# When the output projection's weights are loaded and split: rounds 1 to 5 of the last pair instead of rounds 12 and 13

## The chip, the cores and the metric

The kernel runs on one core of one Trainium2 chip. The metric is device time in microseconds (us) of one execution; of several runs the median is compared. TensorE does the matrix products, VectorE (DVE), ScalarE (ACT) and GpSimd (POOL) the elementwise work, and the sequencer of SyncE (SP) issues nearly all transfers in the order of one queue: an issue that has to wait holds up those behind it.

## The reference

Two branches work on the same `x` of 2048 tokens by 640 features and are mixed by a gate for each token.

```python
g = sigmoid((x * gate_w).sum(-1, keepdims=True))
# A: Fourier mixing, the real part of a DFT over features and then over the sequence
a = einsum("bsd,ed->bse", x, dft_hid_re); b = einsum("bsd,ed->bse", x, dft_hid_im)
A = einsum("ts,bse->bte", dft_seq_re, a) - einsum("ts,bse->bte", dft_seq_im, b)
# B: attention with 32 heads of 20 features, one shared k and v
q = (x @ wq) in 32 heads; k = x @ wk; v = x @ wv
B = concat_heads(softmax(q k^T / sqrt(20)) v) @ wo
out = g * A + (1 - g) * B
```

All data are fp32. The product of this study's concern is the last one of B, `@ wo`, with weights of 640 by 640.

## The kernel before

**Splitting.** Exact products are made out of faster ones: an fp32 operand is split into a rounded high part and the remainder, the low part, and a product becomes three matmuls, high by high, high by low and low by high (`mm3`, L114 to L116). Every operand that is streamed this way has to be split first, by one CAST and one TENSOR_TENSOR.

**Stages.** The kernel first projects `q`, `k`, `v` and the gate, then does the hidden DFT. Then comes the long part: heads are worked through in 16 pairs (`NPAIR`), and between the attention's matmuls TensorE gets those of the sequence DFT. A pair has score maxima (`a`, L330, reduced by VectorE at L337), scores (`b`, L785, with the exponential on ScalarE at L795) and the weighted sum of `v` (`av`, L799). The order of all this is written out as a string, `PLAN`, for 15 pairs. The last pair has no maxima left for a successor, and its order is a loop of 16 rounds, `kk` = 0 to 15. At the end stands the output projection: 32 groups `o_group`, one for each block of 128 tokens and half of the features, 15 matmuls each, with the two weight parts `wos` and the split attention output `ospl`.

**The sequence DFT in the last pair.** It is made of seven products of half-sized matrices (`PRODUCTS`), each in eight groups of output rows, 56 groups `g` in all (`GROUPS`). A group takes the sequence matrix in two halves, `sh` = 0 and 1. For a half, `load_c` fetches a raw block `craw` of 128 by 1024 (two where the product takes a sum) and `split_c` makes `ch` and `cl` of it (L463, L464), on VectorE for groups 49 to 55. Groups 48 to 55 fall into the last pair, one half a round. In the middle of half (g, sh) the half (g+1, sh) is split, two rounds ahead of its use; so round 12 splits (55, 0) and round 13 (55, 1), which TensorE uses in rounds 14 and 15. When a group has ended, ScalarE copies the two sums out (`y_evict`, L685), and GpSimd adds them (L707) and combines them with earlier results (`ya`, L712), which go back to `y_d`.

**The output projection's preparation.** It hangs on a table, `BEFORE`, whose functions are called behind a round:
- `load_wo(cs)`: for each block `c` of 128 rows of `wo`, a load into a buffer `xr0` or `xr1` (by turns, those that the DFT's `load_x` used before), then the CAST and TENSOR_TENSOR on VectorE (L567, L568) into `ab0` to `ab4`, the places of an operand of the product before;
- `load_o(n)`: a quarter of the last pair's half of tokens: attention sums `oT_d` and reciprocal softmax sums `rx_d`; `mult_o(n)` multiplies them on GpSimd (L590); `split_o(n)` splits the result on VectorE (L606, L607);
- `load_y(tb)`: rows of the finished Fourier branch for the mixing, into buffers that `craw`, `ch` and `cl` leave.

**What sets the order.** For TensorE, ScalarE, VectorE and GpSimd the order of issue is the order of the code (`manual_schedule`). SP's queue is not in that list: the framework orders the transfers by its own plan, so a load can stand earlier than its line, and it waits there until its buffer is free. All waits between engines are semaphores.

**The last half's sums.** `finish_half` writes a half's attention sums and softmax sums to memory, `finish_last` reads the softmax sums back, takes the reciprocals on VectorE (L845) and sends them out and in again for `mult_o`.

Of the kernel before, what the change touches and what calls it, by code (L numbers as in the profile page):

```python
# [22 lines left out]
KC = D // P  # L23
NT = S // P
# [10 lines left out]
def kernel(  # L35
# [69 lines left out]
    def move(dst, src, queue=nc.sync):  # L105
        queue.dma_start(words(dst), words(src))  # L106
# [262 lines left out]
    def tick():  # L369
        clock["n"] += 1  # L370
        due = [t for t in todo if t[0] <= clock["n"]]
        todo[:] = [t for t in todo if t[0] > clock["n"]]
        for _, f, args in due:
            f(*args)
# [182 lines left out]
    def spare(k, name):  # L557
        tag, n = SPARE[k % 4]
        return cpools[n].tile([P, D], F32, tag=tag, name=name)

    def load_wo(cs):
        for c in cs:
            raw = xp.tile([P, D], F32, tag=f"xr{c % 2}", name="woraw")
            move(raw, wo[c * P : (c + 1) * P])
            t = abp.tile([P, 2, D], F32R, tag=f"ab{c}0", name=f"wo{c}")
            split_w = (t[:, 0], t[:, 1])
            nc.vector.tensor_copy(split_w[0], raw)  # L567
            nc.vector.tensor_tensor(split_w[1], raw, split_w[0].bitcast(F32), op=ALU.subtract)  # L568
            wos[c] = split_w
# [5 lines left out]
    def load_o(n):  # L575

        if n < NO:
            oraw[n] = []
            for k, v in enumerate((oT_v, rx_v)):
                if (n % 2, k) == (1, 1):  # L580
                    t = op.tile([P, KC, TW], F32, name="oraw", bufs=1)
                else:
                    t = abp.tile([P, KC, TW], F32, tag=f"ab{5 + 2 * (n % 2) + k}0", name="oraw")
                move(t, v[:, :, n * TW : (n + 1) * TW])
                oraw[n].append(t)

    def mult_o(n):
        if n < NO:
            o, r = oraw[n]
            nc.gpsimd.tensor_tensor(o, o, r, op=ALU.mult)  # L590

    def split_o(n):
        if n < NO:
            if n % 4 == 0:

                h, l = [
                    qbuf[(LAST + 1 + k) % 3][:, : KC * TW].rearrange("p (c t) -> p c t", c=KC)
                    for k in range(2)
                ]
            else:  # L600
                h, l = [
                    abp.tile([P, KC, TW], F32R, tag=f"ab{2 * (n % 4 - 1) + k}1", name="osp")
                    for k in range(2)
                ]
            o = oraw.pop(n)[0]
            nc.vector.tensor_copy(h, o)  # L606
            nc.vector.tensor_tensor(l, o, h.bitcast(F32), op=ALU.subtract)  # L607
            ospl[n] = (h, l)

    def load_y(tb):  # L610
        if tb < NT:
            yrow[tb] = spare(tb, "yrow")
            move(yrow[tb], y_d[tb * P : (tb + 1) * P])
# [61 lines left out]
    def y_evict():  # L675

        if not ended:
            return
        grp = ended[0]
        ps = grp["ps"]  # L680
        if "t" not in grp:
            grp["t"] = [op.tile([P, HALF], F32, name=("yt", "yu")[k]) for k in range(len(ps))]
            grp["left"] = list(range(len(ps)))
        k = grp["left"].pop(0)
        nc.scalar.activation(grp["t"][k], ps[k], AF.Copy)  # L685
        if not grp["left"]:
            ended.pop(0)
            y_out(grp)
# [153 lines left out]
    def finish_last(ts, sm):  # L842
# [107 lines left out]
    STEPS = [(p, qh, kc) for p in range(NPAIR) for qh in range(2) for kc in range(NT)]  # L950

    BEFORE = {
        4: (lambda: load_wo(range(3)), lambda: load_o(0), lambda: load_o(1)),
        5: (lambda: load_wo(range(3, KC)), lambda: mult_o(0), lambda: mult_o(1)),
        6: (lambda: split_o(0), lambda: load_o(2)),
        7: (lambda: [load_y(tb) for tb in range(4)],),
    }
    LAG = 2
    taken["V"] = LAG
# [1 line left out]
    def next_b(g, tag):  # L961
        r, nb = divmod(taken["b"][g], 4)
        p, qh, kc = STEPS[2 * r + nb // 2]
        b_unit(p, g, kc, 2 * qh + nb % 2, tag)
        taken["b"][g] += 1
        ready()

    def next_v():
        st = taken["V"] - LAG
        taken["V"] += 1  # L970
        if st >= 0:
            av_step(*STEPS[st])
            if STEPS[st][2] == NT - 1:
                finish_half(*STEPS[st][:2])
# [23 lines left out]
    for kk in range(NT):  # L998
        block = 2 if kk in (0, NT - 1) else 4 * (kk % 2)
        at = (1, 5, 9, 13) if block else (0, 6, 12, 18)  # L1000
        for i in range(24):
            if i in at:
                tick()
                for g in range(2):
                    next_b(g, f"S{lrot % 5}")
                    lrot += 1
            halves.run(0)
            if i == 23:
                y_evict()
            halves.run(1)  # L1010
        y_evict()
        for _ in range(block):
            next_v()
        for f in BEFORE.get(kk - NT // 2, ()):
            f()
    old = STEPS[-LAG:]
    for _ in range(2):
# [6 lines left out]
    for i in range(2 * NT):  # L1024
        tb, e = divmod(i, 2)
# [63 lines left out]
```

## Time and profile before

| what | value |
|---|---|
| median of 3 runs | 1782.73 us (1782.6 to 1783.92) |
| profiled execution | 1780.08 us |
| its span, first to last instruction | 1778.3 us |
| TensorE busy | 1768.7 us, 99% |
| VectorE busy | 1429.6 us, 80% |
| ScalarE busy | 1186.8 us, 67% |
| GpSimd busy | 823.6 us, 46% |
| granted TensorE clock | 1.000 |

Rows of a timeline give the start in us from the span's beginning, the time to the end of the last merged instruction, engine, line, operation, names as output<-input, shapes and count; brackets hold the idle time just before and what ended it. A row of waits gives who waited for whom, the total in us, how often, and the longest. Matmuls are pipelined, so consecutive rows of TensorE overlap. In the last pair the rounds 0 and 1 begin near 1597 us, and every two rounds after them take 12.70 us, but for the last two.

### The profile page before, as it was taken

Reading aid. Unit: us, or ns where it says so; the run is one execution under the profiler, and the core shown is the slowest. Engines: PE = TensorE matmul, PEld = TensorE weight load, DVE = VectorE, ACT = ScalarE, POOL = GpSimd, SP = SyncE. Lnnn points to the kernel's source line nnn. Section 1 sums busy time; section 2 is a strip of 40 time slices with the busy share of each in tenths; the row PEclk is TensorE's granted clock in tenths of the full one; section 3 lists DMA queues with packets and bytes.
Section 4 is the critical chain, followed back from the end, with each engine's and each line's share of the span. In section 5 each row is a group of like instructions: output and inputs, shape, how many; then the busy total and the mean of one; then the engine's idle time right before and its main releaser. Section 6 shows DMA issues by size and latency. Waiting matters only on the chain.

```text
span 1778.3 us, 40733 instructions
## 1 busy us (share of the span) xinstructions
PE 1768.7 (99%) x16342; PEld 1265.7 (71%) x16342; DVE 1429.6 (80%) x2335; ACT 1186.8 (67%) x2327; POOL 823.6 (46%) x559
## 2 busy tenths in 40 slices
PE   9999999999999999999999999999999999999999
PEld 7799986666666666666666666666666666667789
DVE  5479998888888888888888888888888888843364
ACT  5422247777777777777777777777777777777631
POOL 1011127544456464657655556565654444342332
PEclk9999999999999999999999999999999999999999
DMA  8663324342434432535443434342433242325566
GB/s 277 224 196 101 110 98 143 97 131 86 141 110 137 126 126 93 172 117 161 131 162 119 140 113 153 106 152 98 153 122 122 71 144 75 103 73 173 194 216 222
DMA packets 131002, 243.88 MB, mean 137 GB/s; under 512 B 26356, under 2 KB 77556, under 8 KB 128292
## 3 DMA queue, kind: packets, MB, share of 16 engines
q1 hardware_dynamic: 130012, 238.00, 41.5%
q0 software_dynamic: 800, 3.28, 0.6%
q8 instruction: 128, 2.10, 0.5%
q14 instruction: 62, 0.51, 0.1%
HBM read 194.62 MB, written 50.86 MB: 138 GB/s over the span
## 4 chain that ended last, share of the span: by engine, by line
PE 94%; issue 2%; DMA 2%; POOL 1%; DVE 1%; SPq 0%; ACT 0%; POOLq 0%; DVEq 0%; ACTq 0%
PE av L799 26%; PE y L656 19%; PE a L330 17%; PE b L785 16%; PE ab L125 8%; PE o L114 1%; PE q L114 1%; PE q L116 1%; PE o L116 1%; PE o L115 1%; PE q L115 1%; POOL ya L712 1%; DMA craw<-in_cre_dram 0%; DMA y_d<-ya 0%; SPq L106 0%
## 5 line engine op out<-in xcount | busy, mean ns | idle before, releaser
L337 DVE TENSOR_REDUCE mx<-a 128x1 f32<-128x512 f32 x2048 | 1264.6, 681 | 172.1 <-PE a L330 118.2
L795 ACT ACTIVATE pt<-b 128x512 f32<-128x512 f32 x2048 | 1052.3, 620 | 334.7 <-PE b L785 200.0
L656 PE MATMUL y<-x,ch 64*128 64x320 f32 x3584 | 756.6, 309 | 0.7 <-ACT yt L685 0.7
L330 PE MATMUL a<-ks,qs 60*128 60x512 f32 x2048 | 741.0, 423 | 0.3 <-ACT half L533 0.3
L785 PE MATMUL b<-qs,ks 62*128 62x512 f32 x2048 | 712.5, 422 | 0.0
L656 PEld LDWEIGHTS y<-x,ch 64*128 64x128 f32 x3584 | 559.8, 185 | 29.8 <-issue 17.7
L656 PE MATMUL y<-x,cl 64*128 64x320 f32 x1792 | 514.6, 308 | 3.0 <-DVE cl L464 3.0
L799 PE MATMUL av<-pt,vsb 128*32 128x512 f32 x4096 | 502.7, 600 | 0.0
L330 PEld LDWEIGHTS a<-ks,qs 60*128 60x128 f32 x2048 | 350.2, 184 | 135.9 <-DVE mx L337 100.1
L785 PEld LDWEIGHTS b<-qs,ks 62*128 62x128 f32 x2048 | 339.7, 184 | 114.7 <-ACT pt L795 61.3
L656 PEld LDWEIGHTS y<-x,cl 64*128 64x128 f32 x1792 | 308.3, 184 | 6.4 <-DVE cl L464 3.4
L459 POOL TENSOR_TENSOR craw<-craw 128x1024 f32<-128x1024 f32 x80 | 191.4, 2392 | 261.8 <-DMA craw<-in_cre_dram 111.9
L799 PEld LDWEIGHTS av<-pt,vsb 128*32 128x32 f32 x4096 | 108.2, 108 | 200.5 <-issue 179.5
L464 POOL TENSOR_TENSOR cl<-craw,ch 128x1024 fp32r<-128x1024 f32 x98 | 234.5, 2393 | 7.9
L463 POOL CAST ch<-craw 128x1024 fp32r<-128x1024 f32 x98 | 101.7, 1038 | 148.0 <-PE y L656 105.0
L125 PE MATMUL ab<-wh,xh 64*128 64x320 f32 x640 | 144.4, 307 | 0.0
L125 PE MATMUL ab<-wh,xl 64*128 64x320 f32 x640 | 144.1, 305 | 0.0
L125 PE MATMUL ab<-wl,xh 64*128 64x320 f32 x640 | 144.0, 306 | 0.0
L712 POOL TENSOR_TENSOR ya<-yt,ya 128x320 f32<-128x320 f32 x64 | 60.0, 952 | 107.5 <-ACT yt L685 103.5
L125 PEld LDWEIGHTS ab<-wh,xh 64*128 64x128 f32 x640 | 105.7, 185 | 0.0
L533 ACT ACTIVATE half<-ab 128x320 f32<-128x320 f32 x64 | 28.1, 439 | 115.3 <-PE ab L125 115.3
L125 PEld LDWEIGHTS ab<-wl,xh 64*128 64x128 f32 x640 | 97.7, 185 | 0.0
(88 smaller groups left out, 1093.2 us busy)
## 6 DMA issues: line engine op xcount, KB each, us to landing
craw<-in_cre_dram SPq DMA_DIRECT2D x96, 512.0 KB
craw<-in_cim_dram SPq DMA_DIRECT2D x96, 512.0 KB
xr<-x_d SPq DMA_DIRECT2D x88, 320.0 KB
qs<-qh_d SPq DMA_DIRECT2D x64, 160.0 KB
x_d<-both SPq DMA_DIRECT2D x64, 160.0 KB
ya<-y_d SPq DMA_DIRECT2D x64, 160.0 KB
y_d<-ya SPq DMA_DIRECT2D x64, 160.0 KB
xr<-in_xT_dram SPq DMA_DIRECT2D x20, 256.0 KB
```

The lines of the kernel that those rows point to most:

```text
L114: nc.tensor.matmul(ps, wh, xh, start=(i == 0), stop=False)
L125: nc.tensor.matmul(ps, w[r], x[r], start=(i == 0 and k == 0), stop=(i == n - 1 and k == 2))
L330: nc.tensor.matmul(ps, qs[p][b : b + 60, qb * P : (qb + 1) * P], ks[b : b + 60, c * ROW : (c + 1) * ROW], start=True, stop=True,)
L337: return nc.vector.tensor_reduce(mx[p][:, hh, qb, c : c + 1], ps, axis=AX.X, op=ALU.max)
L459: eng.tensor_tensor(raw, raw, raws[1], op=PRODUCTS[n][0][1])
L463: eng.tensor_copy(h, raw)
L464: eng.tensor_tensor(l, raw, h.bitcast(F32), op=ALU.subtract)
L656: mm = nc.tensor.matmul(ps[g % len(ps)], w, x, start=start, stop=stop)
L712: nc.gpsimd.tensor_tensor(ya, yt, ya, op=how)
L785: nc.tensor.matmul(ps, ks[b : b + 62, kc * P : (kc + 1) * P], qs[p][b : b + 62, qc * ROW : (qc + 1) * ROW], start=True, stop=True,)
L795: halves.scored(nc.scalar.activation(t, ps, AF.Exp, scale=SCALE), n)
L799: nc.tensor.matmul(ps[32 * g : 32 * g + 32, :], vsb[:, kc, :], t, start=first, stop=last)
```

## The change

Each of the five blocks of `wo` now has a call of its own, behind rounds 1, 2, 3, 4 and 5. The table's keys become round numbers; the other entries keep their rounds.

```diff
     BEFORE = {
-        4: (lambda: load_wo(range(3)), lambda: load_o(0), lambda: load_o(1)),
-        5: (lambda: load_wo(range(3, KC)), lambda: mult_o(0), lambda: mult_o(1)),
-        6: (lambda: split_o(0), lambda: load_o(2)),
-        7: (lambda: [load_y(tb) for tb in range(4)],),
+        **{kk: (lambda c=kk - 1: load_wo((c,)),) for kk in range(1, 1 + KC)},
+        12: (lambda: load_o(0), lambda: load_o(1)),
+        13: (lambda: mult_o(0), lambda: mult_o(1)),
+        14: (lambda: split_o(0), lambda: load_o(2)),
+        15: (lambda: [load_y(tb) for tb in range(4)],),
     }
...
-        for f in BEFORE.get(kk - NT // 2, ()):
+        for f in BEFORE.get(kk, ()):
             f()
```

On VectorE, in rounds 12 and 13, these rows stood between the splits of (55, 0), the first two rows, and of (55, 1), the two that follow; `wo_...` is one block's split weights, `woraw` its raw load:

```order
 L463 CAST ch<-craw 128x1024
 L464 TENSOR_TENSOR cl<-craw,ch 128x1024
-L567 CAST wo_27320<-woraw 128x640
-L568 TENSOR_TENSOR wo_27320<-woraw,wo_27320 128x640
-L567 CAST wo_27325<-woraw 128x640
-L568 TENSOR_TENSOR wo_27325<-woraw,wo_27325 128x640
-L567 CAST wo_27330<-woraw 128x640
-L568 TENSOR_TENSOR wo_27330<-woraw,wo_27330 128x640
 L463 CAST ch<-craw 128x1024
 L464 TENSOR_TENSOR cl<-craw,ch 128x1024
```

The split of (55, 1) now follows that of (55, 0) directly; the two blocks that came behind it are gone as well. On VectorE, in rounds 1 to 3, one block comes in behind each sequence-matrix split, beginning with that of (49, 1), the first two rows (rounds 4 and 5 go on in the same way):

```order
 L463 CAST ch<-craw 128x1024
 L464 TENSOR_TENSOR cl<-craw,ch 128x1024
+L567 CAST wo_26188<-woraw 128x640
+L568 TENSOR_TENSOR wo_26188<-woraw,wo_26188 128x640
 L463 CAST ch<-craw 128x1024
 L464 TENSOR_TENSOR cl<-craw,ch 128x1024
+L567 CAST wo_26285<-woraw 128x640
+L568 TENSOR_TENSOR wo_26285<-woraw,wo_26285 128x640
 L463 CAST ch<-craw 128x1024
 L464 TENSOR_TENSOR cl<-craw,ch 128x1024
+L567 CAST wo_26401<-woraw 128x640
+L568 TENSOR_TENSOR wo_26401<-woraw,wo_26401 128x640
```

So the weights of block 0 stand between the splits of (49, 1) and (50, 0), and so on to block 4 between (51, 1) and (52, 0). In SP's queue the loads of blocks 0 and 1 stood early before and still do; those of blocks 2, 3 and 4 move here, behind the writes of the half's sums from `ob` (`ya` and `y_d` are the DFT's earlier results, `sm` softmax sums):

```order
+L106 DMA woraw<-in_wo_dram 128x640
+L106 DMA sm<-sum_d 128x32
+L106 DMA y_d<-ya 128x320 x2
+L106 DMA craw<-in_cre_dram 128x1024
+L106 DMA ya<-y_d 128x320 x2
+L106 DMA woraw<-in_wo_dram 128x640
+L106 DMA craw<-in_cre_dram 128x1024
+L106 DMA woraw<-in_wo_dram 128x640
```

Before, these three loads stood in rounds 13 and 14, two of them ahead of a pair of `ya` and one behind it. The order of TensorE, ScalarE and GpSimd is the same in both kernels.

## The prediction

> **What bounds the kernel now.** I read the page first, then the waits of TensorE, then the last 180 us engine by engine. The page says that TensorE is busy nearly all the time and that the chain that ended last runs on it:
>
> ```profile
> span 1778.3 us, 40733 instructions
> PE 1768.7 (99%) x16342; PEld 1265.7 (71%) x16342; DVE 1429.6 (80%) x2335; ACT 1186.8 (67%) x2327; POOL 823.6 (46%) x559
> ...
> PE 94%; issue 2%; DMA 2%; POOL 1%; DVE 1%; SPq 0%; ACT 0%; POOLq 0%; DVEq 0%; ACTq 0%
> ```
>
> The change adds and removes no matmul and leaves TensorE's order alone, so it can only act on the places where TensorE stands still. The view of the waits, for TensorE over the whole span, has one large entry after the start-up, and it stands first:
>
> ```profile
> PE y L656 <- DVE cl L464: 3.0, 1, 3.0
> ...
> PE y L656 <- ACT yt L685: 0.7, 1, 0.7
> ```
>
> It is a single wait of 3.0 us for VectorE's low part of a sequence-matrix block. The timeline of TensorE places it in round 15 of the last pair, and shows where the output projection begins:
>
> ```profile
> 1692.91 0.31 PE L656 MATMUL y<-x,ch 64*128 64x320 f32 x2
> 1696.24 0.41 PE L656 MATMUL y<-x,cl 64*128 64x320 f32 x2 [3.02 <-DVE cl L464]
> ...
> 1700.39 1.92 PE L799 MATMUL av<-pt,vsb 128*32 128x512 f32 x16
> 1702.25 0.42 PE L114 MATMUL o<-wo,qs 128*128 128x320 f32 x1
> ```
>
> What it costs in all is read from two windows that hold the same work, from one batch of `av` matmuls to the next: rounds 12 and 13, and rounds 14 and 15.
>
> ```profile
> core 0: us, PE busy (x) PEld busy (x) DVE busy (x) ACT busy (x) POOL busy (x), PEclk, DMA share, GB/s
> 1671.69:1684.39 12.70, 12.70 (x146) 9.52 (x145) 3.89 (x6) 9.10 (x19) 2.55 (x3) 1.00 0.67 216
> 1684.39:1700.39 16.00, 12.98 (x146) 9.50 (x144) 13.64 (x11) 9.26 (x19) 9.63 (x5) 1.00 0.47 145
> ```
>
> Both have 146 matmuls at a granted clock of 1.00. One takes 12.70 us, the other 16.00, so the disturbance is worth 16.00 - 12.70 = 3.30 us: the 3.02 of standing still and some 0.3 of getting going again.
>
> Why was VectorE late? Its timeline ahead of that moment:
>
> ```profile
> 1680.32 0.69 DVE L463 CAST ch<-craw 128x1024 fp32r<-128x1024 f32 x1 [9.89 <-DMA craw<-in_cre_dram]
> 1681.12 1.22 DVE L464 TENSOR_TENSOR cl<-craw,ch 128x1024 fp32r<-128x1024 f32 x1
> 1682.27 0.49 DVE L567 CAST wo<-woraw 128x640 fp32r<-128x640 f32 x1
> ...
> 1686.99 0.57 DVE L567 CAST wo<-woraw 128x640 fp32r<-128x640 f32 x1 [2.12 <-DMA woraw<-in_wo_dram]
> 1687.59 1.37 DVE L568 TENSOR_TENSOR wo<-woraw,wo 128x640 fp32r<-128x640 f32 x1
> 1688.89 3.46 DVE L463 CAST ch<-craw 128x1024 fp32r<-128x1024 f32 x1
> 1692.45 3.74 DVE L464 TENSOR_TENSOR cl<-craw,ch 128x1024 fp32r<-128x1024 f32 x1
> ```
>
> The first two rows split block (55, 0). Then three splits of the projection's weights run, the third after a wait of 2.12 us for its load. Only then comes block (55, 1), and its two instructions take 3.46 + 3.74 us in place of 0.69 + 1.22. GpSimd shows what they met:
>
> ```profile
> 1688.24 6.87 POOL L590 TENSOR_TENSOR oraw<-oraw 128x1280 f32<-128x1280 f32 x2
> 1732.79 2.98 POOL L590 TENSOR_TENSOR oraw<-oraw 128x1280 f32<-128x1280 f32 x1 [17.74 <-DMA oraw<-rx_d]
> ```
>
> The two products of `mult_o` ran from 1688.24 to 1695.11, and the slow pair lies over them; VectorE finished 1.1 us after GpSimd. So the wait has two halves: the weights pushed (55, 1) from 1682.3 to 1688.89, and there it fell on `mult_o`.
>
> **The change part by part.** *Removed from rounds 12 and 13:* ten VectorE instructions and three loads (the first two loads stood early in SP's queue already). The rows of the weights' tile, durations as least, median, most:
>
> ```profile
> L567 DVE CAST wo<-woraw x5: 480/485/569, 1682.3 to 1697.4; 128x640 fp32r<-128x640 f32 x5
> L568 DVE TENSOR_TENSOR wo<-woraw,wo x5: 824/826/1371, 1682.8 to 1697.9; 128x640 fp32r<-128x640 f32 x5
> ```
>
> One block costs 0.485 + 0.826 = 1.31 us. With them gone, (55, 1) follows (55, 0) at 1682.3, if its raw block is there. SP issued both raw blocks by then, that of (55, 1) first, when the split of (54, 0) let its buffer go:
>
> ```profile
> 1668.52 0.34 SPq L106 DMA_DIRECT2D craw<-in_cre_dram  x1
> 1672.89 0.52 SPq L106 DMA_DIRECT2D craw<-in_cre_dram  x1
> ```
>
> The second landed at 1680.3 and released the split of (55, 0), so the first should be in. At the unhindered 0.69 + 1.22 us, (55, 1) is ready at about 1684.3. TensorE wants it at about 1693.06 (0.15 us behind 1692.91): 8.8 us to spare, and GpSimd's `mult_o` starts only at 1688.24. The whole 3.30 us goes.
>
> *Added to rounds 1 to 5:* the same ten instructions, one block behind each split of (49, 1) to (51, 1). VectorE's rows there, with the idle time before each in brackets:
>
> ```profile
> 1604.80 0.69 DVE L463 CAST ch<-craw 128x1024 fp32r<-128x1024 f32 x1
> 1605.59 1.23 DVE L464 TENSOR_TENSOR cl<-craw,ch 128x1024 fp32r<-128x1024 f32 x1
> 1611.11 1.25 DVE L463 CAST ch<-craw 128x1024 fp32r<-128x1024 f32 x1 [4.29 <-POOL ya L712]
> ...
> 1616.37 0.69 DVE L463 CAST ch<-craw 128x1024 fp32r<-128x1024 f32 x1 [2.68 <-PE y L656]
> ...
> 1621.77 0.70 DVE L463 CAST ch<-craw 128x1024 fp32r<-128x1024 f32 x1 [3.38 <-DMA craw<-in_cre_dram]
> ...
> 1629.08 0.69 DVE L463 CAST ch<-craw 128x1024 fp32r<-128x1024 f32 x1 [4.81 <-PE y L656]
> ...
> 1634.42 0.69 DVE L463 CAST ch<-craw 128x1024 fp32r<-128x1024 f32 x1 [3.33 <-DMA craw<-in_cre_dram]
> ```
>
> The five gaps are 4.29, 2.68, 3.38, 4.81 and 3.33 us; each takes 1.31 and keeps at least 1.37. If a block runs over all the same, the next cover is the two rounds by which splits run ahead. TensorE starts on group 49 here:
>
> ```profile
> 1612.08 0.46 PE L656 MATMUL y<-x,ch 64*128 64x320 f32 x4
> ```
>
> Block (49, 0) was ready before (49, 1) began at 1604.80, 7.3 us ahead. So VectorE could be some 7 us late before TensorE felt it. I charge nothing; the bounds are 0 and, were all five splits wholly on the path, 5 x 1.31 = 6.6 us.
>
> *The loads on SP's queue:* five issues move. Their rows of before:
>
> ```profile
> 1600.80 0.90 SPq L106 DMA_DIRECT2D woraw<-in_wo_dram  x2
> ...
> 1611.01 0.27 SPq L106 DMA_DIRECT2D oT_d<-ob  x1
> ...
> 1683.64 1.59 SPq L106 DMA_DIRECT2D woraw<-in_wo_dram  x2
> ```
>
> A load lands some 3.3 us after issue (1683.64 to the third split at 1686.99). Blocks 0 and 1 go out near 1600.8 as before, some 6 us ahead of the split at 1606.8. Block 2 waits for the split of block 0 (done about 1608.2) and stands behind the last row of `ob`; issued near 1611.4 it is there by 1614.8, and its split comes at 1618.4. Block 4 must wait for that split, to about 1619.7, and is wanted at 1631.1. While SP waits, the gated loads `ya` and `craw` queue behind; they have the same 7 us and more. In rounds 13 and 14 SP loses three issues and their waits, so `yrow`, `y_d` and the second operand of `mult_o(2)` go out sooner. None is on TensorE's path: a gain of 0.
>
> *What is late next.* TensorE reaches the first output group 3.3 us earlier, at 1702.25 - 3.30 = 1698.95, and needs `split_o(0)`, which waits for `mult_o(0)`: 1688.24 + 2.98 = 1691.2. A cast of that size beside a running `mult_o` has a row, and the first group of the second half of the tokens has two:
>
> ```profile
> 1712.15 3.58 DVE L606 CAST osp<-oraw 128x1280 fp32r<-128x1280 f32 x1 [0.30 <-POOL oraw L590]
> ...
> 1736.66 1.49 DVE L607 TENSOR_TENSOR qs<-oraw,qs 128x1280 fp32r<-128x1280 f32 x1
> 1739.60 0.31 PE L114 MATMUL o<-wo,qs 128*128 128x320 f32 x1
> ```
>
> With 3.58 + 1.49 us, `split_o(0)` ends at about 1696.3, 2.7 us before it is wanted; unhindered it would end at 1693.5. The Trainium skill, "SBUF — State Buffer", section "Who interferes with whom", says that VectorE and GpSimd share one pair of ports under an exclusive lock, and that the loser blocks for the other's whole instruction. By that rule both instructions may have to wait out `mult_o(1)`, and the sum stays the same with the slack near 2 us; the rows of (55, 1) agree with a loser that blocks. That is why giving something back gets more than a few hundredths below.
>
> Sum: 1778.3 - 3.3 + 0 = 1775.0 of span, or 1780.08 - 3.3 = 1776.8 for that execution. The runs shown have a median of 1782.73, 2.65 above it; I take the same saving off the median: **1779.4 us**, -0.19%. What a measurement of this kernel can tell from no change is about 0.2%, 3.6 us, so the forecast lies 0.3 us inside that line.
>
> **The rivals.** *More than 3.3 us (0.07).* A wait just over 3 us might cost speed afterwards. If the rest of round 15 ran at half clock, 1696.24 to 1700.39, 4.15 us, would be the worth of another 4.15, and the gain up to 7.45: 1775.3. Against it: the clock is 1.00 in the window and 146 matmuls take 12.98 us of busy time. The Trainium skill, "TensorE: Matmul & The Clock Gate", Part 1, halves the clock after an idle window of about 3.4 us. By that rule a wait of 3.02 us may fall just short here and just over in other executions; the trace shows only the former.
>
> *Something given back, or less there to gain (0.13).* The second half's chain of sums, from the last `av` through SP's queue to `split_o(4)`, ends at 1736.66 + 1.49 = 1738.15, only 1.45 us before TensorE needs it at 1739.60. If it did not move with TensorE, 1.85 of the 3.30 would return: 1781.3. It starts from TensorE's own last `av`, so I expect it to move. Or (55, 1) starts 0.65 us earlier in executions without a profile, ahead of 1688.24, and there is less of a wait to remove: down to no gain, 1782.7.
>
> *Slower (0.08).* In rounds 1 to 5 a weight block at the head of VectorE's queue lands late; the split behind it and, through the buffers, SP's next loads wait, and TensorE runs dry at the start of a group. It decides once VectorE is over 7.3 us late; to outweigh 3.3 and reach 0.2% it must lose TensorE 6.9 us, 14 in all. All five splits on the path give 1779.4 + 6.6 = 1786.0, and with a little waiting for loads 1786.3 or more. Against it: gaps of 2.68 us and more, loads of 3.3.
>
> **How the numbers follow.** The forecast has 0.72. The runs before spread over 1.3 us, more than the 0.3 that part it from 0.2%, so half of it (0.36) falls on either side. Faster: 0.36 + 0.07 = 0.43; within: 0.36 + 0.13 = 0.49; slower 0.08. The range takes the spread around 1779.4 down to 1778.0, and up into the second rival to 1781.8.
>
> **What would show it.** Right: no wait of TensorE on `cl` in round 15; (55, 1) directly behind (55, 0) with about 0.7 and 1.2 us; rounds 14 and 15 in 12.7 us; the weights' splits in rounds 1 to 5 inside VectorE's gaps. Wrong: a wait of TensorE on `cl` in rounds 2 to 7, on `split_o(0)` at the first output group, or on `split_o(4)` near 1736.

## The result and the profile after

| | before | after |
|---|---|---|
| median of 8 runs each | 1783.24 us (1782.6 to 1783.92) | 1778.49 us (1777.75 to 1778.94) |
| first profile: time, span | 1780.08, 1778.3 | 1778.74, 1777.0 |

The ratio is 0.9973, with a 95% interval of 0.9962 to 0.9983: faster by 4.75 us in the medians, where 3.3 were forecast. The two first profiles differ by only 1.34 us, so this pair of profiles does not tell the gain by itself.

The waits of TensorE over the whole span, after. The one for `cl` is gone, and no other has taken its place:

```profile
PE kv L210 <- DVE kvgs L110: 1.6, 1, 1.6
PE warm L244 <- POOL ident masks.py:199: 1.4, 1, 1.4
PE y L656 <- ACT yt L685: 0.7, 1, 0.7
PE a L330 <- ACT half L533: 0.3, 1, 0.3
```

Windows of rounds 12 and 13 and of rounds 14 and 15, after; the columns are those of the prediction's windows:

```profile
1673.65:1686.35 12.70, 12.70 (x146) 9.52 (x144) 3.30 (x4) 9.10 (x19) 2.55 (x3) 1.00 0.65 204
1686.35:1699.06 12.71, 12.71 (x147) 9.56 (x145) 6.42 (x5) 9.13 (x19) 8.41 (x5) 1.00 0.74 239
```

Both take the same now. VectorE there, after: (55, 1) directly behind (55, 0), nothing in between, and `split_o(0)` beside `mult_o`:

```profile
1682.85 0.69 DVE L463 CAST ch<-craw 128x1024 fp32r<-128x1024 f32 x1 [10.36 <-DMA craw<-in_cre_dram]
1683.64 1.23 DVE L464 TENSOR_TENSOR cl<-craw,ch 128x1024 fp32r<-128x1024 f32 x1
1684.79 0.68 DVE L463 CAST ch<-craw 128x1024 fp32r<-128x1024 f32 x1
1685.58 1.23 DVE L464 TENSOR_TENSOR cl<-craw,ch 128x1024 fp32r<-128x1024 f32 x1
1692.95 3.58 DVE L606 CAST qs<-oraw 128x1280 fp32r<-128x1280 f32 x1 [6.15 <-POOL oraw L590]
1696.56 1.49 DVE L607 TENSOR_TENSOR qs<-oraw,qs 128x1280 fp32r<-128x1280 f32 x1
```

What the profile of after loses elsewhere is at the start. The windows view of its first 5 to 12 us:

```profile
5.00:12.00 7.00, 5.43 (x16) 3.65 (x16) 4.40 (x7) 3.79 (x6) 0.28 (x1) 0.76 1.01 381
```

It waited 1.6 us for the first loads, where before had waited 0.8, and ran at a clock of 0.76. It began the last pair's matmuls on group 48 at 1598.89, before at 1596.92, with the same instructions up to there. Over the fourteen profiles of this study, the batch of `av` ahead of round 14 begins between 1684.20 and 1686.35, whatever the kernel. So parts of a profile are compared below from that batch on.

### The profile page after: what moved, and what is told of

Same layout as the page of the kernel before. It is cut to its first block, busy times and chain, and to the rows that moved or that the text cites. A ratio compares the mean times of both kernels' runs of the same rounds, so it can differ in the third digit from the quotient of the medians.

```text
span 1777.0 us, 40732 instructions
## 1 busy us (share of the span) xinstructions
PE 1769.7 (100%) x16342; PEld 1266.6 (71%) x16342; DVE 1424.1 (80%) x2335; ACT 1186.8 (67%) x2327; POOL 821.4 (46%) x559
## 4 chain that ended last, share of the span: by engine, by line
PE 99%; DMA 0%; ACT 0%; DVE 0%; issue 0%; SPq 0%; ACTq 0%
PE av L799 27%; PE y L656 22%; PE a L330 17%; PE b L785 17%; PE ab L125 8%; PE q L114 1%; PE q L116 1%; PE o L114 1%; PE q L115 1%; PE o L115 1%; PE o L116 1%; PE kv L210 0%; PE kv L211 0%; DMA kvg<-in_wkvg_dram 0%; PE kvt L231 0%
## 5 line engine op out<-in xcount | busy, mean ns | idle before, releaser
L125 PE MATMUL ab<-wh,xh 64*128 64x320 f32 x640 | 137.4, 307 | 0.0
L125 PE MATMUL ab<-wl,xh 64*128 64x320 f32 x640 | 137.3, 306 | 0.0
L125 PE MATMUL ab<-wh,xl 64*128 64x320 f32 x640 | 137.0, 305 | 0.0
L125 PEld LDWEIGHTS ab<-wh,xl 64*128 64x128 f32 x640 | 100.3, 184 | 0.0
```

Source lines behind the costliest of these rows:

```text
L125: nc.tensor.matmul(ps, w[r], x[r], start=(i == 0 and k == 0), stop=(i == n - 1 and k == 2))
```

## The experiments

### One part alone: blocks 0 to 2, and blocks 3 and 4

The first kernel is after with blocks 3 and 4 put back behind round 13, the second is after with blocks 0, 1 and 2 put back behind round 12.

```diff
-        **{kk: (lambda c=kk - 1: load_wo((c,)),) for kk in range(1, 1 + KC)},
+        **{kk: (lambda c=kk - 1: load_wo((c,)),) for kk in range(1, 4)},
...
-        13: (lambda: mult_o(0), lambda: mult_o(1)),
+        13: (lambda: load_wo(range(3, KC)), lambda: mult_o(0), lambda: mult_o(1)),
```

```diff
-        **{kk: (lambda c=kk - 1: load_wo((c,)),) for kk in range(1, 1 + KC)},
-        12: (lambda: load_o(0), lambda: load_o(1)),
+        **{kk: (lambda c=kk - 1: load_wo((c,)),) for kk in range(4, 1 + KC)},
+        12: (lambda: load_wo(range(3)), lambda: load_o(0), lambda: load_o(1)),
```

> One part of the change: only blocks 0, 1 and 2 move to rounds 1 to 3, blocks 3 and 4 stay behind round 13. Theory (the three blocks of round 12 push the split of (55, 1) into mult_o): they alone carry the change, so no wait on cl, rounds 14 and 15 in 12.7 us, and the time of after, 1778.5 (ratio 0.9973). Rival (the total of VectorE work late in the pair matters, so each block counts): three fifths of the gain, about 1780.4.

> The other part alone: blocks 3 and 4 move to rounds 4 and 5, blocks 0, 1 and 2 stay behind round 12. Theory: they stand behind (55, 1) in VectorE's queue, so nothing is gained: the wait of 3.0 us stays, rounds 14 and 15 take 16.0 us, 1783.2 (ratio 1.000). Rival (each block counts): two fifths of the gain, about 1781.3.

Blocks 0 to 2 early: 1776.94 us against 1782.77 of before on the same chip, ratio 0.9973 (0.9962 to 0.9984). Blocks 3 and 4 early: 1783.69, ratio 1.0005 (0.9996 to 1.0014). The three blocks ahead of (55, 1) carry the whole change; taking work off VectorE behind it shows no gain. The second kernel waits as before, but longer than the 3.0 us, and 16.0 us for the two rounds, that were expected: TensorE waits 3.2 us for `ch` and 0.5 for `cl`, and rounds 14 and 15 take 18.51 us at a clock of 0.91:

```profile
1685.14:1703.65 18.51, 14.77 (x147) 10.93 (x145) 14.30 (x11) 9.49 (x19) 9.09 (x5) 0.91 0.45 133
```

VectorE in the first of them shows that splits under `mult_o` (GpSimd, 1689.28 to 1695.99) are harmless where nobody waits for them. Blocks 3 and 4 now take the slow place, behind (55, 1):

```profile
1685.58 1.92 DVE L464 TENSOR_TENSOR cl<-craw,ch 128x1024 fp32r<-128x1024 f32 x1
...
1689.93 3.24 DVE L567 CAST wo<-woraw 128x640 fp32r<-128x640 f32 x1
1693.20 3.46 DVE L568 TENSOR_TENSOR wo<-woraw,wo 128x640 fp32r<-128x640 f32 x1
1696.59 0.82 DVE L606 CAST qs<-oraw 128x1280 fp32r<-128x1280 f32 x1
1697.44 1.49 DVE L607 TENSOR_TENSOR qs<-oraw,qs 128x1280 fp32r<-128x1280 f32 x1
```

`split_o(0)` was done at 1698.93, and TensorE began the output at 1699.10: just in time.

### The weights left late, `mult_o` off GpSimd

```diff
-            nc.gpsimd.tensor_tensor(o, o, r, op=ALU.mult)
+            (nc.vector if n < 2 else nc.gpsimd).tensor_tensor(o, o, r, op=ALU.mult)
```

> Before, with the two products of mult_o(0) and mult_o(1) on VectorE (behind the weights' blocks 3 and 4) in place of GpSimd; the weights stay in rounds 12 and 13. Theory (the lateness alone would be harmless, it is the meeting with mult_o on GpSimd that makes it a wait): (55, 1) starts as late as before, 1688.9, but takes 0.7 + 1.2 us, is ready near 1690.9, 2 us ahead of TensorE; no wait, rounds 14 and 15 in 12.7 us, the time of after. Rival (VectorE is simply too late, the shared ports are a side effect): a wait of 1 us or more stays, 1780.5 to 1782.

It took 1777.56 us, ratio 0.9973 (0.9964 to 0.9982): the whole gain with every weight split still in round 12 or 13. VectorE of this kernel, and its rounds 14 and 15:

```profile
1687.68 1.03 DVE L567 CAST wo<-woraw 128x640 fp32r<-128x640 f32 x1 [2.11 <-DMA woraw<-in_wo_dram]
1688.74 0.82 DVE L568 TENSOR_TENSOR wo<-woraw,wo 128x640 fp32r<-128x640 f32 x1
1689.49 0.69 DVE L463 CAST ch<-craw 128x1024 fp32r<-128x1024 f32 x1
1690.28 1.23 DVE L464 TENSOR_TENSOR cl<-craw,ch 128x1024 fp32r<-128x1024 f32 x1
...
1684.72:1697.42 12.70, 12.70 (x146) 9.56 (x144) 10.36 (x12) 9.13 (x19) 2.56 (x3) 1.00 0.53 154
```

The reload wait of 2.11 us is there as before, and (55, 1) starts 4.8 us behind the batch of `av` at 1684.72 (in before 4.5 behind 1684.39). It takes 0.69 and 1.23 us and TensorE does not wait. The lateness was harmless; its meeting with `mult_o` cost the time. One of the 11 executions took 1781.87 us, at a mean granted clock of 0.999 where the other ten had 1.000; it has no profile.

### A third raw buffer

```diff
-            raw = xp.tile([P, D], F32, tag=f"xr{c % 2}", name="woraw")
+            raw = xp.tile([P, D], F32, tag=f"xr{c % 2 if c != 2 else 2}", name="woraw")
```

> Before, with a third buffer for the raw weights, so that block 2 need not wait for block 0's buffer; all five blocks stay in rounds 12 and 13. Theory (it is the reload of 2 to 2.8 us that brings (55, 1), or the block ahead of it, under mult_o): the three splits run back to back, (55, 1) starts some 4 us behind (55, 0)'s end, at the time at which mult_o starts or before, and is ready at least 1 us ahead of TensorE; no wait, 1778.5. Rival (three splits between are enough to be caught): the wait stays at 3 us or more, 1782.8.

It took 1779.9 us, ratio 0.9989 (0.9980 to 0.9998), between the two. Its profile has no wait in round 15, and a new one at the first output group. The waits of TensorE, first row, and the windows from round 14's `av` to the end of round 15 and on to the second output group:

```profile
PE o L116 <- DVE qs L607: 1.4, 1, 1.4
...
1685.81:1698.52 12.71, 12.71 (x147) 9.57 (x145) 12.54 (x8) 9.14 (x19) 10.63 (x5) 1.00 0.72 225
1698.52:1704.45 5.93, 4.51 (x34) 2.62 (x32) 5.76 (x6) 2.23 (x5) 4.85 (x3) 1.00 0.60 189
```

The second window is 4.25 us in after (two batches of `av`, 1699.06 and 1703.31), so 1.7 were given back: block 3 fell under `mult_o` in place of (55, 1), block 4 came behind it, and `split_o(0)` ended at 1702.29. In this profile the theory holds for the reload. For the price it was half right: the queue behind (55, 1) had its own user waiting. Three of the 11 executions (1780.74, 1782.63 and 1786.81 us) had a mean clock of 0.998 or 0.999, the others 1.000; what happened in those three no profile shows.

### Before, three times more

Unchanged copies of before, one timed beside it (1782.51 us, ratio 1.0001, 0.9992 to 1.0010; the profiled execution took 1785.8) and two as single profiled executions (1784.83 and 1784.98 us).

> The kernel before, unchanged, profiled and timed a second time. The first profile of before took 1780.08 us, all its other runs 1782.6 to 1783.92; and the profile of after begins its last pair 1.96 us later than that of before (first matmuls at 6.63 in place of 6.26 us, then some at 0.63 us each). Theory A (the first profile of before had a quick start, the wait is the same in all runs): ratio 1.000, this profile has the wait of TensorE on cl at 3.0 us and 16.0 us for rounds 14 and 15, and reaches the last pair some 2 us later than the first one did. Theory B (the wait is longer or followed by a slow clock in ordinary runs): the last pair begins as before, rounds 14 and 15 take 17.3 us or more.

> Before, unchanged, one more profile. Rounds 14 and 15 took 16.00 us in the first profile of before and 19.76 in the second. Theory (VectorE's last weight split comes under mult_o as well in ordinary runs, and a slow clock follows): 17.5 to 20 us, TensorE waiting for ch and then for cl, at a clock under 0.95 in those two rounds. Rival (the second profile was the odd one): 16.0 us, a wait for cl alone, clock 1.00.

> Before, unchanged, a fourth profile, for the same question: 17.5 to 20 us for rounds 14 and 15 by the theory, 16.0 by the rival.

Rounds 14 and 15 of the three, in the windows view:

```profile
1686.34:1706.10 19.76, 16.01 (x146) 12.10 (x144) 17.88 (x16) 9.50 (x19) 9.86 (x5) 0.83 0.59 177
```

```profile
1685.40:1705.12 19.72, 15.82 (x147) 11.73 (x145) 18.59 (x17) 9.48 (x19) 9.77 (x5) 0.83 0.56 171
```

```profile
1686.24:1705.29 19.05, 16.05 (x146) 11.95 (x144) 17.45 (x15) 9.48 (x19) 9.62 (x5) 0.82 0.59 180
```

Against 12.70 they lose 7.06, 7.02 and 6.35 us, and the first profile's 3.30 was the least of the four. Their times, 1784.8 to 1785.8 us, lie above the median of 1782.5 as the first one's lies below it, so none of the four is a typical run by its time. The mean granted clocks of all executions of before that ran beside the experiments say more: 61 of 67 had 0.998 or 0.999, and the six with 1.000, like the first profile, took 1780.2 to 1781.6 us. Of the 31 executions of four kernels without the wait (blocks 0 to 2 early, `mult_o` off GpSimd, after again, longer warm-up) 30 had 1.000. (After's first eight runs had 0.999 four times; a start like that of its profile, 0.76 over 7 us, gives as much by itself.) So most executions of before lose something to a lower clock, and the first profile is one of the few that do not.

Both theories of the first copy had a share in the truth: its last pair began 1.95 us later (1598.87 for 1596.92), and its rounds 14 and 15 were longer. The theory of the other two came out in time and clock, but not in its waits: TensorE waited once, for `ch`, 3.89 and 3.00 us, and not for `cl` behind it. TensorE in the second profile of before, around the wait and in the slow stretch behind it:

```profile
1697.89 0.41 PE L656 MATMUL y<-x,ch 64*128 64x320 f32 x2 [3.25 <-DVE ch L463]
1698.14 0.40 PE L785 MATMUL b<-qs,ks 62*128 62x512 f32 x2
1698.38 0.34 PE L656 MATMUL y<-x,ch 64*128 64x320 f32 x2
1699.22 0.64 PE L656 MATMUL y<-x,cl 64*128 64x320 f32 x2 [0.51 <-DVE cl L464]
```

A pair of `y` matmuls that took 0.31 us before the wait takes 0.47 to 0.64 after it, up to about 1705.4. The granted clock from 1698.7 to 1705.4 is 0.50, and it is 0.50 too for 5.7 and 6.4 us behind the wait in the other two. VectorE and GpSimd of the same profile say why (55, 1) came later still:

```profile
1691.09 3.46 DVE L568 TENSOR_TENSOR wo<-woraw,wo 128x640 fp32r<-128x640 f32 x1
1694.47 3.37 DVE L463 CAST ch<-craw 128x1024 fp32r<-128x1024 f32 x1
1697.94 1.23 DVE L464 TENSOR_TENSOR cl<-craw,ch 128x1024 fp32r<-128x1024 f32 x1
```

```profile
1690.61 6.68 POOL L590 TENSOR_TENSOR oraw<-oraw 128x1280 f32<-128x1280 f32 x2
```

Here the second half of block 2's split was the first to be held by `mult_o`, (55, 1)'s CAST the second, and `cl` came after both: one instruction later than in the first profile. In the third profile of before both instructions of block 2's split were held, and (55, 1) itself ran at its full speed behind them, too late:

```profile
1690.21 3.31 DVE L567 CAST wo<-woraw 128x640 fp32r<-128x640 f32 x1 [0.71 <-DMA woraw<-in_wo_dram]
1693.55 3.39 DVE L568 TENSOR_TENSOR wo<-woraw,wo 128x640 fp32r<-128x640 f32 x1
1696.86 0.68 DVE L463 CAST ch<-craw 128x1024 fp32r<-128x1024 f32 x1
```

### Filling matmuls in the place of the wait

```diff
+FILL = 14
...
+        if kk == NT - 1:
+            fill = bank(f"S{lrot % 5}", "fill")
+            lrot += 1
+            for _ in range(FILL):
+                nc.tensor.matmul(fill[:, :P], ident, ident, start=True, stop=True)
```

> Before, with 14 matmuls of the identity by itself, that nothing reads, put into TensorE's queue at the start of round 15, where it stands still; all else as before. Theory (in ordinary runs of before the stand-still of over 3.4 us is followed by a stretch at a lower granted clock, 2 us or more of the loss, which the first profile did not show): TensorE is busy in place of idle, the clock stays at 1.00, rounds 14 and 15 take 16.0 to 16.8 us, the runs' clocks are 1.000, and the time is 1780.5 to 1781.5, faster than before by 1.3 to 2.3 us although work was added. Rival (the clock has no part, the extra loss is more waiting): no faster than before, or slower by up to 0.5 us.

> The kernel with filling matmuls in round 15, once more: its first profile had the clock at 1.00 and rounds 14 and 15 in 16.7 us, but its median of 1782.62 showed no gain over before. Theory (a second wait, for VectorE's split_o at the first output group, takes the gain in the slower runs): a wait of TensorE at the output projection of 1 us or more, when the time is over 1782.5. Rival (longer waits at round 15 in spite of the filling): rounds 14 and 15 at 18 us or more, nothing at the output.

> The same kernel as the run before, a third profile: a wait at the output group of 1 us or more by the theory if it is over 1782.5, rounds 14 and 15 at 18 us or more by the rival.

The three profiles have rounds 14 and 15 at a clock of 1.00:

```profile
1685.19:1701.91 16.72, 16.49 (x174) 12.70 (x172) 14.43 (x13) 9.27 (x19) 9.57 (x5) 1.00 0.50 156
```

```profile
1685.89:1702.75 16.86, 16.52 (x175) 12.71 (x173) 15.12 (x13) 9.27 (x19) 9.69 (x5) 1.00 0.52 152
```

```profile
1684.30:1700.64 16.34, 16.34 (x174) 12.69 (x172) 14.11 (x12) 9.16 (x19) 9.19 (x5) 1.00 0.50 148
```

VectorE is nearly as late as in before's later profiles (`cl` is done 12.2 to 12.7 us behind the batch of `av` in these three, 12.6 to 13.5 there), but the two rounds take 16.3 to 16.9 us in place of 19.0 to 19.8. From the end of `cl` to the end of round 15 it is 4.2 us here and in the first profile of before, and 6.2 to 6.9 in its three later ones. So 2.0 to 2.7 us of their loss of 6.35 to 7.06 is the lower clock that follows an idle TensorE, and 4.1 to 5.0 is VectorE's lateness, where the first profile had 3.30 of lateness alone.

All 11 timed runs had a clock of 1.000, where before's had 0.998 to 1.000. And yet the median was 1782.62, ratio 0.9999 (0.9990 to 1.0008): the forecast of a faster kernel failed, though the interval, from 1.8 us faster to 1.4 us slower, leaves room for the lower part of its 1.3 to 2.3. The two further profiles bear out neither explanation that was offered: the execution that took 1783.03 waited only 0.2 us for `split_o`, and its rounds 14 and 15 took 16.86 us. It needed some 0.6 us more after round 15 than the others and began round 14 late, at 1685.89; that is not enough for the slower runs, up to 1784.35. What they lose is open, and so the median is no witness for the clock's share; the profiles are.

### After again, and with a longer warm-up

```diff
-WARM = 9
+WARM = 12
```

> After, unchanged, beside the others. Theory (all that is left of differences between its runs is the start): rounds 14 and 15 in 12.7 us, no wait on cl, ratio 0.9973 within its interval; runs whose clock is below 1.000 are those with a slow start, like the first profile of after (0.76 in its first 5 to 12 us).

> After, with 12 in place of 9 warm-up matmuls at the start, to keep TensorE busy until the first loads are there. Theory (the slow start of some runs comes from the idle time of 0.4 to 1.6 us ahead of the first projection): the idle time shrinks to under 0.5 us, the clock is 1.00 in 5 to 12 us, and the median falls by 0.3 to 0.8 us below after's, to 1777.7 to 1778.2. Rival (the start is set by the loads alone): the same time as after.

After took 1777.45 us beside them, ratio 0.9973 (0.9962 to 0.9983). Its rounds 14 and 15 took 12.70 (1684.20 to 1696.90). All eight executions had a clock of 1.000, so its expectation on slow starts was not put to the test. With 12 warm-up matmuls it was 1776.88, ratio 0.9968 (0.9955 to 0.9980). The five runs lie closer together (1776.41 to 1777.17) than after's eight (1776.62 to 1778.92), and the idle time at the start was 0.3 us. But the profile of after had a good start as well this time, 0.4 us, with a clock of 1.00. The intervals overlap; that the longer warm-up gains is likely, not shown. No kernel here had a lower median.

## Why the prediction was right, and where it was short

**What bounds it, and what the wait was made of.** Right, and shown. The two halves that the prediction named were pulled apart: moving blocks 0 to 2 alone removes the wait, and so does taking `mult_o` off GpSimd while they stay. Either is enough.

**Rounds 12 and 13.** Right: (55, 1) ran in 0.68 + 1.23 us directly behind (55, 0), done at 1686.8, some 8 us ahead of TensorE.

**Rounds 1 to 5.** Right that nothing of it reaches TensorE. The cover was thinner than said. In before the first `craw` was split 5.9 us after the last pair began (1602.86 and 1596.92), in after 7.8 us (1606.66 and 1598.89). Much of that is a difference between executions and not the change: the first split came 5.8 to 7.2 us after the pair's start in kernels with before's order of loads, and 6.0 to 7.8 in the four with blocks 0 to 2 early. The prediction let five loads move in SP's queue; those of blocks 0 and 1 stay near the front, but block 0's now goes out 0.5 us behind that `craw`, ahead of two `ya`, and in before 1.8 us behind it. Whether this adds anything is not shown. In this profile of after (49, 0) was ready some 5.4 us ahead of its use, where 7.3 had been counted, and the splits slid along, still inside the gaps; the least idle time left was 0.74 us, where 1.37 had been counted.

**What is late next.** Right: `split_o(0)` took 3.58 + 1.49 us and ended at 1698.05, 2.9 us before the output began at 1700.91 (2.7 were forecast). The second half's chain was done at 1733.53 and TensorE wanted it at 1738.26, 4.7 us of slack in place of 1.45: `split_o(2)` no longer collides with `mult_o` and lets the reciprocal through earlier (1714.78 in place of 1718.09, of which 1.3 is the shift of the whole stage).

**The step that was short** is the sum's one term, 16.00 - 12.70 = 3.30 us. As a reading of that profile it was exact. As the worth of the wait in ordinary runs it was too small: three further profiles put it at 6.35 to 7.06, the kernel with blocks 3 and 4 early, which has the same queue ahead of (55, 1), at 5.81, and the medians at 4.75 (the result), 5.0 (after again) and 5.8 (blocks 0 to 2 early). What it left out is a later VectorE and, in most executions, a lower clock. The term should have been a range, from the profile's 3.30 up to the 7.45 of the rival. That the time came so near, 1778.49 for 1779.4, is in part luck: the gain was 1.45 us larger than forecast, but the median of before that it was taken off rose by 0.51 us, from 1782.73 of three runs to 1783.24 of eight.

**The rivals.** "More than 3.3 us" came true as a mechanism and got only 0.07: in the three later profiles of before the clock behind the wait is 0.50, the half that it had assumed, for 5.7 to 6.7 us; it cost 2.0 to 2.7 us, where 4.15 had been put. The argument against it, a clock of 1.00 in one window, told of one execution only. The Trainium skill, "TensorE: Matmul & The Clock Gate", Part 1, says that the clock is halved after an idle window of about 3.4 us, and that the window runs freely. The traces agree with the half, 0.50. They do not agree with 3.4 us as a least length of the gap, and a wait near 3 us went either way: 3.02 us was followed by 1.00, and 3.00 us in the last profile of before by 0.50. "Less there to gain" named the right switch, 0.65 us between VectorE and `mult_o`, and the wrong side of it: in the other profiles of before VectorE met `mult_o` one or two instructions earlier in its queue, and TensorE waited for `ch`. "Slower" did not happen; no wait appears in rounds 2 to 7.

**The median against the profile.** The first profile of before was 2.65 us under the median of its first three runs. The prediction wrote that down and took the same saving off both. A part of the 2.65 can be the start of the kernel, which differs by up to 2 us between profiles; the rest was a sign that this execution lost less in the very place that was being priced.

## What to carry to other kernels

A small late job does harm not by its length but by what it pushes into: look along the in-order queue behind it for an instruction that shares something with another engine, and for the user that waits for that one. Price a wait over several executions, or as a range, when the profiled time differs from the median, above all a wait near 3 us on TensorE, behind which the clock may fall; the mean granted clock of the timed runs shows whether it does. When a job is moved out, check who inherits the place: with the third buffer it was the next split in the queue, and its user waited in turn.

## What the runs showed of the hardware that was not expected

- A TensorE idle for 3.0 to 3.9 us was followed by a stretch at a granted clock of 0.50 in three of four profiles of before, for 5.7 to 6.7 us, with matmuls 1.5 to 1.6 times as long (0.47 for 0.31 us a pair, 0.63 for 0.40). With 3.4 us of filling matmuls in that place the clock stayed at 1.00 in all three profiles.
- Beside two `mult_o` in a row (5.9 to 7.1 us together) VectorE got about one instruction through for each of them, 3.0 to 3.7 us a piece, whatever its size: 128 by 640, 1024 or 1280.
